# Attention and MLP on one core: a new written-out order of all work, and dummy matmuls of 256 columns

## The chip, the cores and the metric

The kernel runs on one core of a Trainium2 chip. The metric is the device time of one execution in microseconds (us). The core has five engines with instruction streams of their own: TensorE (PE in the profile, with its weight loads shown apart as PEld), VectorE (DVE), ScalarE (ACT), GpSimd (POOL) and SyncE (SP), which here only issues transfers. Transfers run on 16 DMA engines that all issuing engines share.

## The reference

```python
def phi(x):                          # sketch features, r = 8, so 64 of them
    a = einsum('rd,bhsd->bhsr', S1, x)
    b = einsum('rd,bhsd->bhsr', S2, x)
    return einsum('bhsi,bhsj->bhsij', a, b).reshape(*x.shape[:-1], r * r)

q_p, k_p = phi(q), phi(k)            # q, k, v: 4 batches, 4 heads, 1088 positions, 32 wide
kv  = einsum('bhsf,bhsd->bhfd', k_p, v)
z   = sum(k_p, axis=2)
num = einsum('bhsf,bhfd->bhsd', q_p, kv)
den = einsum('bhsf,bhf->bhs', q_p, z)[..., None] + 1e-06
x   = (num / den) as 4352 tokens x 128
h   = x @ w_in                       # 128 -> 2048
g   = maximum(h, 0) + alpha * minimum(h, 0)
out = g @ w_out                      # 2048 -> 128
```

Inputs and output are float32.

## The kernel before, in words

The kernel is one straight line of some 750 named steps (`Op`), each with an engine, and all of them stand in one string, `ORDER` (lines 23 to 67). A word such as `r0.4:a:2` says: step r0.4, on ScalarE (a; p is PE, d VectorE, g GpSimd, s SyncE), with buffer slot 2. A number behind the letter p (`rowsT:p4:6`) makes PE run so many dummy matmuls ahead of the step (`dummy`, line 293; called at line 781): 128 columns of ones, into a PSUM bank that nobody reads. `warm` (line 289) is 13 such matmuls of 256 columns at the very start. `arrange` (line 95) walks through ORDER; each engine takes its steps in that order, so ORDER decides what waits behind what. Each engine waits for the data and for the buffers that a step needs: PSUM has eight banks, "rh" (the activated hidden values) eight slots, "oT" (results on their way out) six.

The steps, by the names that follow:

- Loads: `ld_...` on SP, the four slices of w_in on GpSimd, and the small S1, S2, alpha on ScalarE. q and k come a batch at a time (544 KB), v in four parts per batch (`ld_v1`, `ld_v1_1` and so on), w_out in four slices. `winT0` to `winT3` (line 395) are transposing transfers of w_in inside the core.
- Weights: rowsT, Wk, Wf, S2m, S2q, Ssd prepare the sketch matrices; `w_a`, `w_b`, `w_hi`, `w_lo` scale and split w_out; `Wmm0` to `Wmm3` (line 404) multiply them with winT into W. The MLP is computed as relu(x w_in) times w_out (1 - alpha), plus x W.
- Keys of batch b: `k1T0` transposes, `k1f0` (line 491) makes features, `k1fT0` transposes back, `k1p0` and `k1p1` (helper at line 195) form the 64 products, `zs10` (line 517), `z11`, `zS1`, `C1` sum them up, `kv10` (line 530; batch 0: kv00 to kv04, line 546) multiplies them with v, `kvc1`, `fin1` (line 423) and `kvR1` lay the result out.
- Queries: batch 0 is split. Its first 512 columns take a short way of their own (`qaT`, `qaf` line 643, `qas`, `den` and `num` line 653, `dT`, `rc`, `rr`, `xA`). The rest, and batches 1 to 3, go through `qbT`/`q1T0`, `qbf`/`q1f` (line 448), `..fT`, `..t`, `..rc`, `..b`, `..p0`, `..p1`, `..PT0`, `..PT1`, `qbn`/`q1n` (line 607) and `..x0`, `..x1`, which write x.
- MLP: eleven groups of tokens (0, 1, 8, 9 and 10 have 256, the others 512). `h2.5` (line 702) is the matmul of group 2 with w_in slice 5, `r2.5` (ScalarE line 708 or VectorE line 710) evicts it with a relu, `o2.5` (line 723) multiplies with w_out, `W2` closes the sum (`D0` to `D2` do the x W part of groups 0 to 2 apart), `oT2` transposes the result, `st2` stores it (line 746: four transfers; line 753: eight). Group 10 is stored by `st10.0` on SP and `st10.1` on ScalarE (line 759).

A 256-token hidden step shares one eviction between two slices (r0.4 is for h0.4 and h0.5). Each PE matmul is two instructions, a weight load and a matmul; a matmul with float32 operands is passed through twice, so four. `qbn` for example has 128 instructions, `kv10` 144, a step h or o two.

## Time and profile before

| | us |
|---|---|
| runs of the kernel | 111.35, 111.72, 114.65 (median 111.72) |
| the profiled execution, time of its own | 112.21 |
| its span (first to last instruction) | 110.2 |
| PE busy in the span | 96.7 |
| VectorE, ScalarE, GpSimd busy | 80.5, 70.2, 46.7 |
| DMA: read and written in HBM | 8.80 MB, 2.23 MB |

The span is 2.0 us shorter than the execution, which has a start and an end around it. All engines overlap, so the busy times do not add up. Most loads fall in the first 36 us; the page's slices show the DMA engines full there, and nearly idle from 40 to 60 us. PE has 1401 weight loads (PEld) and 1401 matmuls. Start times below are counted from the span's start; a matmul's duration in the trace includes its way through the array, so that the spacing of starts is the price of one in a row.

### The profile page before, as it was taken

What the parts mean: (1) busy time and instruction counts of PE and PEld (TensorE: products, weight loads), DVE (VectorE), ACT (ScalarE), POOL (GpSimd) and SP (SyncE); (2) the same over time, 40 slices, a digit from 0 to 9 for tenths busy, and PEclk for the clock granted to TensorE, in tenths of its full rate; (3) what the DMA queues carried; (4) which work ended last, traced back from release to release, by engine and by line L of the source; (5) the groups of instructions that cost most, each with busy time, mean ns of one, the idle gap of its engine ahead of it and who ended that gap; (6) DMA issues with size and microseconds to landing.
All of it is one profiled execution on the core that took longest, in us unless ns stands there. A gap on an engine that the chain in (4) does not pass through costs nothing.

```text
span 110.2 us, 3417 instructions
## 1 busy us (share of the span) xinstructions
PE 96.7 (88%) x1401; PEld 56.5 (51%) x1401; DVE 80.5 (73%) x135; ACT 70.2 (64%) x150; POOL 46.7 (42%) x51
## 2 busy tenths in 40 slices
PE   7999999999169699999999999999999999999100
PEld 5638744687144346465444443446544466889100
DVE  4997979999349896997999978999946363857100
ACT  3304357989619779679679667395929979766000
POOL 7499009897205999370077039469300000000000
PEclk9999999999999999999999999999999999999955
DMA  3999999999999900000000500500112640551220
GB/s 68 300 258 270 238 295 312 239 143 295 239 180 312 77 6 0 6 0 0 6 0 0 95 0 6 95 1 6 24 30 38 120 81 3 98 102 32 44 43 23
DMA packets 26231, 11.25 MB, mean 102 GB/s; under 512 B 19928, under 2 KB 25064, under 8 KB 26216
## 3 DMA queue, kind: packets, MB, share of 16 engines
q1 hardware_dynamic: 25396, 10.43, 45.1%
q0 software_dynamic: 576, 0.52, 3.1%
q8 instruction: 11, 0.18, 0.7%
q10 hardware_dynamic: 244, 0.08, 0.3%
q14 instruction: 4, 0.03, 0.2%
HBM read 8.80 MB, written 2.23 MB: 100 GB/s over the span
## 4 chain that ended last, share of the span: by engine, by line
PE 71%; SPq 7%; issue 6%; DVE 5%; DMA 4%; ACT 1%; ACTq 0%; DVEq 0%
PE ps L723 23%; PE ps L702 23%; PE ps L607 5%; SPq L746 3%; PE ps L530 3%; SPq L753 3%; DMA k<-in_k_dram 3%; PE ps L448 2%; PE ps L491 2%; PE ps L546 2%; PE ps L517 2%; PE ps L643 2%; PE ps L404 2%; DMA out_dram<-oT__92 1%; PE ps L295 1%
## 5 line engine op out<-in xcount | busy, mean ns | idle before, releaser
L702 PE MATMUL ps<-x,w_in_bf 128*128 128x512 bf16 (+1 forms) x176 | 42.7, 331 | 0.5 <-DVE x L667 0.5
L702 PEld LDWEIGHTS <-w_in_bf 128*128 128x128 bf16 x176 | 16.9, 98 | 13.1 <-issue 1.1
L723 PEld LDWEIGHTS <-w_a_bf 128*128 128x128 bf16 x160 | 15.2, 98 | 15.6 <-issue 5.2
L195 POOL TENSOR_TENSOR P__71<-Fk__69 128x512 f32<-128x512 f32 (+3 forms) x7 | 12.1, 1747 | 5.4 <-DVE Fk__69 L496 5.4
L708 ACT ACTIVATE rh__84<-ps 128x512 bf16<-128x512 f32 x14 | 8.4, 597 | 3.8 <-PE ps L702 3.3
L723 PE MATMUL ps<-rh__85,w_a_bf 128*128 128x512 bf16 (+1 forms) x22 | 7.0, 331 | 3.2 <-issue 3.2
L708 ACT ACTIVATE rh__87<-ps 128x512 bf16<-128x512 f32 x13 | 7.9, 610 | 2.9 <-PE ps L702 2.0
L708 ACT ACTIVATE rh__83<-ps 128x512 bf16<-128x512 f32 x14 | 8.5, 605 | 1.6 <-PE ps L702 1.6
L708 ACT ACTIVATE rh__85<-ps 128x512 bf16<-128x512 f32 x14 | 8.4, 603 | 1.5 <-PE ps L723 1.2
L708 ACT ACTIVATE rh__86<-ps 128x512 bf16<-128x512 f32 x12 | 7.2, 600 | 1.9 <-PE ps L723 1.1
L723 PE MATMUL ps<-rh__83,w_a_bf 128*128 128x512 bf16 (+1 forms) x24 | 7.4, 335 | 0.0
L723 PE MATMUL ps<-rh__82,w_a_bf 128*128 128x512 bf16 (+1 forms) x21 | 7.3, 349 | 0.0
L708 ACT ACTIVATE rh__88<-ps 128x512 bf16<-128x512 f32 x10 | 6.1, 608 | 1.6 <-PE ps L702 1.2
L723 PE MATMUL ps<-rh__86,w_a_bf 128*128 128x512 bf16 (+1 forms) x21 | 7.0, 350 | 0.0
L708 ACT ACTIVATE rh__89<-ps 128x512 bf16<-128x512 f32 x11 | 6.7, 606 | 0.1
L708 ACT ACTIVATE rh__82<-ps 128x512 bf16<-128x512 f32 x11 | 6.7, 606 | 0.1
L195 POOL TENSOR_TENSOR P__71<-F__68 128x1152 f32<-128x1152 f32 x2 | 4.3, 2172 | 5.6 <-DVE F__68 L195 5.6
L195 POOL TENSOR_TENSOR w_hl<-w_b_f,w_hl 128x512 bf16<-128x512 f32 x4 | 5.8, 1473 | 1.8 <-ACT Wf L188 1.8
L727 DVE STREAM_TRANSPOSE oT__90<-ps 128x256 f32<-128x256 f32 (+1 forms) x4 | 2.3, 584 | 5.8 <-PE ps L723 5.8
L723 PE MATMUL ps<-rh__84,w_a_bf 128*128 128x256 bf16 (+1 forms) x20 | 6.2, 327 | 0.0
L607 PE MATMUL ps<-Q__74,kvR 32*32 32x288 f32 (+1 forms) x256 | 6.1, 385 | 0.0
L195 POOL TENSOR_TENSOR P__72<-F__67 128x640 f32<-128x640 f32 (+1 forms) x3 | 5.9, 1982 | 0.2
(176 smaller groups left out, 202.9 us busy)
## 6 DMA issues: line engine op xcount, KB each, us to landing
v<-in_v_dram SPq DMA_DIRECT2D x12, 144.0 KB, 6.8
k<-in_k_dram SPq DMA_DIRECT2D x3, 544.0 KB, 6.2
q<-in_q_dram SPq DMA_DIRECT2D x3, 544.0 KB
w_out_f<-in_moe_w_out_dram SPq DMA_DIRECT2D x4, 256.0 KB, 9.0
w_in_bf<-in_moe_w_in_dram POOLq DMA_DIRECT2D x4, 128.0 KB, 7.1
out_dram<-oT__90 SPq DMA_DIRECT2D x8, 64.0 KB, 1.9
v<-in_v_dram SPq DMA_DIRECT2D x4, 112.0 KB, 7.6
out_dram<-oT__93 SPq DMA_DIRECT2D x5, 64.0 KB, 1.9
```

The source lines that it names most:

```text
L195: (nc.vector if e == "dve" else nc.gpsimd).tensor_tensor(out=dst, in0=a, in1=b, op=what)
L404: nc.tensor.matmul(ps(bw)[:, :2 * DM], winT[:, c], w_hl[:, c].rearrange("p y m -> p (y m)"), start=c == 0, stop=c == NC - 1)
L448: nc.tensor.matmul(ps(bf)[32 * g:32 * g + 32, h, :n], Wf[32 * h:32 * h + 32, b], src[1]()[32 * h:32 * h + 32, g * n:(g + 1) * n], start=Tr ...
L491: nc.tensor.matmul(ps(bf)[32 * g:32 * g + 32, u, :n], Wk[K].rearrange("p x f -> p (x f)"), src[1]()[K, g * n:g * n + n], start=True, stop= ...
L530: nc.tensor.matmul(ps(bk)[32 * h:32 * h + 32, :R], v_sb[b][:, h, j], bview(sb(P), [[1, R]], (4 * j + h) * R), start=j == 0, stop=j == JG - ...
L607: nc.tensor.matmul(ps(bn)[32 * h:32 * h + 32, g, :n], kvR[b][32 * g:32 * g + 32, y, 32 * h:32 * h + 32], bview(sb(Q)[32 * g:32 * g + 32], ...
L702: nc.tensor.matmul(ps(b)[:, n * y:n * y + n], w_in_bf[:, c], x(), start=True, stop=True)
L708: nc.scalar.activation(sb(br), ps(b), ACTF.Relu)
L723: nc.tensor.matmul(ps(bo)[:, :n], w, y(), start=c == 0, stop=c == (NC - 1 if later else NC))
L727: o = op({"dve": V(n) + 40}, lambda e: nc.vector.transpose(sb(boT).rearrange("p j f -> p (j f)")[:, :n], ps(bo)[:, :n]), [last], [bo, boT] ...
L746: nc.sync.dma_start(bass.AP(tensor=out.tensor, offset=(b * S + lo // 32) * DM + 32 * i, ap=[[NJ * DM, 32], [DM, n // 32], [1, 32]]), t[32 ...
L753: nc.sync.dma_start(bass.AP(tensor=out.tensor, offset=(32 + y) * DM + 32 * i, ap=[[NJ * DM, 32], [S * DM, B], [1, 32]]), bview(t[32 * i:32 ...
```

## The change: ORDER is replaced, and dummies go in pairs

No step is added or removed apart from dummies, and no tile, shape or dependency is changed. The order in which the steps stand, the engine of 78 of them and the buffer slots are new. The dummy matmuls asked for fall from 16 to 9, and two of 128 columns are now one of 256:

```diff
     def dummy(n=1):
-        for _ in range(n):
-            nc.tensor.matmul(PS[:, 7, :128], ones(128), ones(128), start=True, stop=True, skip_group_check=True)
+        for i in range(0, n, 2):
+            m = 128 * min(2, n - i)
+            nc.tensor.matmul(PS[:, 7, :m], ones(128), ones(m), start=True, stop=True, skip_group_check=True)
```

Whole lines of the old and the new ORDER, from the parts that the prediction speaks of:

```diff
-ld_v0_3:s E8:d ld_alpha:a rowsT:p4:6 ld_qa1:s S2m:p:5 k0T0:d:0 Wk:a ld_qb:s ld_k1:s k0T1:d k0f0:p:0 gate:g ld_w_in0:g Wf:d M4:d qaT0:d ld_w_in1:g
-k0f1:p ld_w_out1:s S2q:d Ssd:d ld_w_in2:g ld_w_out0:s k0fT0:d:0 qaf0:p6:2 ld_w_in3:g k0fT1:d ld_w_out2:s zs00:p:6 k0p0:d:0 zs01:p ld_v1_2:s z10:a:0
-k0p1:d qas0:a zS0:p6 ld_v1:s kv00:p:1 k0p2:g zA:d:0 ld_w_out3:s qaT1:d zfin:p:0 C0:a kv01:p ld_q1:s zc:d:0 qaf1:p:2 qbT:d k0p3:g den0:p:6 ld_v1_1:s
+ld_v0_2:s k0T0:d:0 ld_v0_3:s rowsT:p4:6 ld_qa1:s Wk:d Wf:a gate:g k0T1:d I4:g k0f0:p4:0 ld_qb:s Ssd:d ld_w_in0:g ld_k1:s selP:d k0f1:p qaT0:d
+ld_w_in1:g ld_w_out1:s ld_w_in2:g qaf0:p:2 ld_v1_3:s k0fT0:d:0 ld_w_in3:g k0fT1:d ld_w_out0:s k0p0:d:0 ld_v1_2:s S2m:p1:6 qas0:a zs00:p:1 ld_q1:s
+k0p1:d zs01:p kv00:p:0 ld_v1_1:s k0p2:g zA:d:0 S2q:d kv01:p qaT1:d ld_v1:s zfin:p:6 qbT:d qaf1:p:2 k0p3:g zc:d:0 kv02:p ld_w_out2:s qas1:a k1T0:d:0
...
-zS1:p o0.10:p o0.11:p o1.5:p r1.14:a:6 C1:d o1.6:p o1.7:p k2T0:d:1 q1f:p:0 w_a3:a qbp1:g kv10:p:6 q1fT:d:1 r1.12:a:3 winT1:s o1.8:p o0.12:p o1.9:p
-kvc1:a:0 o1.10:p qbPT1:d o1.11:p w_hi1:a o0.13:p q1t:g:0 o1.12:p o1.13:p o1.14:p ld_v2_3:s o1.15:p w_b0:a fin1:p oT1:d:0 qbn:p:0 ld_q2:s q1rc:d:0
+ld_k3:s h1.0:p:4 r0.14:a:4 ld_q2:s qbrc:d:0 zs10:p:3 h1.1:p r0.12:a:5 o0.0:p:7 o0.1:p r0.6:d:6 ld_v2_2:s o0.2:p o0.3:p z11:a:0 h1.2:p:6 r1.0:a:7
+h1.3:p o0.4:p o0.5:p qbb:d r0.10:a:0 o0.6:p q1T0:d:0 o0.7:p qbp1:g:1 zS1:p h1.4:p:5 kv10:p:4 C1:a w_b2:a w_a2:g qbPT1:d:0 q1f:p:0 r1.2:a:1 kvc1:d:0
+qbp0:g w_hi2:a h1.5:p q1fT:d:1 fin1:p r1.4:a:3 h1.6:p:6 h1.7:p o0.8:p o0.9:p kvR1:a h1.8:p:5 r1.6:a:6 h1.9:p h1.10:p:4 qbPT0:d h1.11:p q1t:g:0
+h1.12:p:3 r1.8:a:2 h1.13:p winT1:s h1.14:p:2 h1.15:p o1.0:p:6 o0.10:p w_a3:g o1.1:p o0.11:p q1rc:d:0 o1.2:p o1.3:p r1.10:a:7 o1.4:p o1.5:p o1.6:p
+ld_v3_3:s r1.14:a:0 k2T0:d:0 w_b0:g o0.12:p o1.7:p r1.12:a:1 o0.13:p o1.8:p o1.9:p o1.10:p w_b3:a o0.14:p o0.15:p o1.11:p o1.12:p q1b:d o1.13:p
+qbn:p:0 oT0:d:0 q1p0:g:0 w_hi0:a k2f0:p:4 qbx0:d qbx1:a winT2:s h2.0:p:3 k2fT0:d:0 h2.1:p:2 q1p1:g h2.2:p:1 r2.0:a:1 h2.3:p:0 r2.2:d:2 h2.4:p:5
```

SP's transfers, old and new order, with the parts of v left under one name where they stand together: before k0, qa0, v0, qa1, qb, k1, w_out1, w_out0, w_out2, v1_2, v1, w_out3, q1, v1_1, v1_3, k2, v2_2, winT0, v2, v3_2, k3, winT1, v2_3, q2, winT2, v3, v3_3, q3, v2_1, winT3, v3_1, then the stores st3, st4, st1, st5, st2, st0, st6 to st10.0; after k0, qa0, v0, qa1, qb, k1, w_out1, v1_3, w_out0, v1_2, q1, v1_1, v1, w_out2, w_out3, k2, winT0, k3, q2, v2_2, winT1, v3_3, winT2, winT3, v3, v3_2, q3, v2_1, v2, v2_3, st2, st3, v3_1, st4, st5, st0, st1, st6 to st10.0.

Steps that change their engine, in the parts spoken of: Wk, C0, kvc1, qbb, k2p1, w_hi1, w_lo1 and w_hi3 go to VectorE, Wf, r0.0 and C1 to ScalarE, k2p0 and I4 to GpSimd.

## The prediction

> **What bounds the kernel now.** I read the page first, then a table of the span in stages, then TensorE's waits, then its instructions around each wait, then the DMA queues, and last SyncE's stores. In the rows of the stage table the columns after the stretch and its length are busy time (and instructions) of PE, PEld, DVE, ACT, POOL, then granted clock, DMA share and GB/s.

> ```profile
> PE 96.7 (88%) x1401; PEld 56.5 (51%) x1401; DVE 80.5 (73%) x135; ACT 70.2 (64%) x150; POOL 46.7 (42%) x51
> ...
> 16.43:28.07 11.64, 11.39 (x255) 7.78 (x255) 10.98 (x18) 10.47 (x28) 10.10 (x9) 1.00 1.22 248
> 28.07:31.23 3.16, 0.00 (x1) 0.00 (x0) 0.34 (x1) 1.25 (x5) 0.49 (x1) 1.00 1.00 249
> 31.23:38.25 7.02, 6.04 (x129) 3.17 (x128) 6.27 (x11) 4.96 (x10) 4.06 (x2) 1.00 1.16 184
> 38.25:102.40 64.15, 64.15 (x799) 35.72 (x798) 49.84 (x68) 47.56 (x95) 23.45 (x16) 1.00 0.19 32
> 102.40:110.20 7.80, 0.00 (x0) 0.00 (x0) 0.29 (x1) 0.27 (x1) 0.00 (x0) 0.66 0.18 37
> ```

> TensorE has no idle time from 38.25 to 102.40, and 0.25 us of it in the 11.64 us before 28.07. What is left is one hole of 3.16 us, one of 0.98 us (7.02 less 6.04), the start, and 7.8 us of stores behind the last matmul. PE ends when its work plus its holes are done. Both holes are put down to "issue", that is to nothing that another engine did:

> ```profile
> PE ps L723 <- issue: 3.2, 1, 3.2
> PE ps L517 <- issue: 1.0, 1, 1.0
> ...
> 23.91 0.27 PE L723 MATMUL ps<-rh__88,w_a_bf 128*128 128x256 bf16 x1
> 31.23 0.27 PE L723 MATMUL ps<-rh__85,w_a_bf 128*128 128x256 bf16 x1 [3.16 <-issue]
> 38.25 0.26 PE L517 MATMUL ps<-Fk__69 128*32 128x16 f32 x8 [0.98 <-issue]
> ...
> q8 instruction: 11, 0.18, 0.7%
> ```

> When is a block asked for? If it is when PE enters the block before, then 692 (o0.8, the row at 23.91) to 31.23 is 7.3 us and 31.23 to 38.25 is 7.0 us. The DMA view counts PE's packets of that time in the stretches 19.2 to 19.3, 27.9 to 28.0 and 35.4 to 35.5:

> ```profile
> q8 instruction: 1, 0.02, 88.8%
> ...
> q8 instruction: 1, 0.02, 115.4%
> ...
> q8 instruction: 1, 0.02, 81.7%
> ```

> So a packet shows 4.0 and 4.2 us after the crossing, and PE goes on 3.3 and 2.85 us after that. All this lies in the time in which the DMA engines are full (share 1.00 to 1.22).

> **Prices.**

> ```profile
> 15.46 0.71 PE L565 MATMUL ps<-kv0W,I 64*128 64x128 f32 x4
> 16.43 0.38 PE L702 MATMUL ps<-x,w_in_bf 128*128 128x256 bf16 x2 [0.27 <-DVE x L667]
> 17.31 0.57 PE L448 MATMUL ps<-qTb,Wf 32*32 32x160 f32 x32
> 19.02 1.25 PE L702 MATMUL ps<-x,w_in_bf 128*128 128x256 bf16 x10
> 21.39 0.50 PE L517 MATMUL ps<-Fk__69 128*32 128x16 f32 x36
> 25.27 0.77 PE L448 MATMUL ps<-T__64,Wf 32*32 32x288 f32 x32
> 25.97 1.23 PE L530 MATMUL ps<-P__71,v 128*32 128x64 f32 x72
> 31.86 1.27 PE L607 MATMUL ps<-Q__74,kvR 32*32 32x160 f32 x64
> 33.06 0.72 PE L491 MATMUL ps<-T__65,Wk 64*32 64x288 f32 x16
> 33.83 0.38 PE L702 MATMUL ps<-x,w_in_bf 128*128 128x512 bf16 x1
> 34.16 1.89 PE L702 MATMUL ps<-x,w_in_bf 128*128 128x512 bf16 x8
> ```

> From start to start: a 256-column matmul 0.109, a 512-column one 0.215; qbf 0.5, q1f 0.7, k2f0 0.65, zs 0.45, kv 1.16 (144 instructions), qbn 1.2 (128 instructions). The short ones are what empties a block fast: kv10 alone is over half a block in 1.16 us.

> **The change, part by part.**

> *Where the blocks end.* Counting the new ORDER the same way gives 2780 instructions (5 dummy matmuls for 16). I keep the bounds at the same numbers. Bound 436 is then at the start of qbf, 692 a quarter into kv10, 948 in the first tenth of qbn, 1204 near the end of zs20. PE's own work between them:
> 436 to 692: qbf 0.5, num1 0.57 (as den and num in before), 27 matmuls of 256 columns 2.94, zs10 0.45, zS1 0.2, 34/144 of kv10 0.27: 4.9.
> 692 to 948: rest of kv10 0.89, q1f 0.7, fin1 0.2, 33 of 256 columns 3.6, a tenth of qbn 0.1: 5.5.
> 948 to 1204: rest of qbn 1.1, k2f0 0.65, 27 of 512 columns 5.8, 54/72 of zs20 0.34: 7.9.
> Before, the second of these took 4.16 us (23.91 to 28.07), the third 6.04. So q1f and kv10 no longer share a block with little else.

> *The start.* In the chain of waits PE runs on from 5.25 to 13.9, and two groups of six dummies lie in it:

> ```profile
> 5.25 1.22 PE ps L491 x16
> 6.47 0.75 PE ps L295 x6
> ...
> 9.04 0.62 PE ps L295 x6
> ...
> 13.90 0.22 ACT kv0W L557
> ...
> 4.38 0.77 PE L356 MATMUL ps<-rows,selP 16*128 16x128 f32 x2
> 7.15 1.24 PE L643 MATMUL ps<-qTa,Ssd 32*128 32x256 f32 x8
> 11.28 0.71 PE L643 MATMUL ps<-qTa,Ssd 32*128 32x256 f32 x8
> L295 PE MATMUL ps<-const-bfloat16-1.0 x5: 218/281/314, 9.1 to 9.4; 128*128 128x128 bf16 x5
> ```

> Gone are 1.37 us, less 0.1 for the one dummy left there; S2m comes into this stretch (at most 0.5 of its 0.77, the rest overlaps); zS0 goes between num0 and fin0 (0.15). That alone is -0.6. Against it: qaf0 takes 1.17 us at 7.15 and 0.65 at 11.28, and the dummies' records shorten to 218 ns at 9.4, though the granted clock reads 1.00 throughout. So PE came to full speed at 9.4, 4.1 us after its last gap, at 5.25. The dummies that are gone covered the wait of qaf0 for VectorE (qaT0 now stands behind Ssd and selP); I estimate the new gap to end at 6.5, and full speed then at 10.6. Each us at the low speed loses 1 - 0.65/1.17 = 0.44, so 1.25 us cost 0.55. Sum -0.1; bounds -0.6 (no later speed) and +0.8 (3.2 us later). h0.0, at 16.43 before, comes at 16.3; h0.0, h0.1 and den1 stand ahead of qbf as before (17.31 less 16.43), so bound 436 is crossed at 17.2.

> *The blocks.* The block for 692 was asked for at 15.9 before (fourth matmul of fin0), its packet shows at 19.2, 3.3 later, and nothing waited for it. With 3.3 to go on after the packet it needs 6.6; bounds 6.2 (3.3 + 2.85) and 7.5 (4.2 + 3.3). Crossing 692: 17.2 + 6.6 = 23.8. PE's work alone would bring it there at 22.1, but kv10 also waits for k1's products on GpSimd and for evictions, so the wait seen will be about 1. The next block was seen twice, 7.3 and 7.0; I take 7.0: crossing 948 at 30.8, where before had 31.23: **-0.4**. The least would be 23.8 + 5.5 = 29.3. The block for 1204 comes at 37.8, PE needs it at 30.8 + 7.9 = 38.7: no hole, **-1.0**. Cover 0.9; without it the hole is back.

> *Work left after 948.* Before, o0.14, o0.15, o1.13 (3 x 0.109), fin1 (0.2) and a tenth of qbn were still to come there; now they are done: **-0.65**. Everything else behind 948 is the same work.

> *Loads, engines, queues.* The same transfers are issued on the same queues, SP's with k3, q2 ahead of most of v2 and v3; k2, w_out and v1 stay early, and v2 is needed by kv20, some 8 us behind bound 1204, where the DMA share is 0.19. v3_1 goes behind st2 and st3 on SP, with st2 waiting for GpSimd's oA2; only kv30, over 15 us later, needs it. Evictions on VectorE are 37 before and after; w_hi1, w_lo1, w_hi3 and k2p1 go to it, k2p0 leaves it. DVE is at 49.84 of 64.15 us behind 38.25. PE now runs some 2 us ahead there, with less cover: **+0.2** for new waits, bounds 0 and 1.

> *The stores.* W6 comes 2 us earlier, W7 0.3 later, W8 and W9 as before, counted from PE's end. SyncE is busy without a break from st7 on and sets the last store:

> ```profile
> 93.32 1.94 SPq L746 DMA_DIRECT2D out_dram<-oT__90  x4
> 95.37 2.36 SPq L746 DMA_DIRECT2D out_dram<-oT__91  x4
> 97.84 4.46 SPq L753 DMA_DIRECT2D out_dram<-oT__92  x8
> 102.40 3.58 SPq L746 DMA_DIRECT2D out_dram<-oT__90  x4
> ```

> st7, st8, st9 follow one another as before, so the 7.8 us stay: 0.

> Sum: -0.4 - 1.0 - 0.65 + 0.2 = -1.85. The profiled execution took 112.21 us (span 110.2 and 2.0 around it), so 110.4; against the median of the three runs, 111.72, it is **109.9 us**.

> **Rivals.** About 2% is what a measurement of this kernel can tell from no change: 109.5 and 114.0.
> 1. *The blocks come sooner* (bytes in flight differ, no hole left): 17.2 + 4.9 + 5.5, plus 0.25 of small waits as in 16.43 to 28.07, puts 948 at 27.9; -3.3 - 1.65 + 0.2 = -4.8, 107.0. Half of it gives 108.4. For it: the first two packets show after 3.3, not 4. Against: the DMA share is 1.0 and more there. Chance 0.30 for 109.4 and less by this.
> 2. *SyncE's last group shortens.* st9's four stores took 3.58, st6's 1.94; if the 1.64 goes, 108.2. No rule for it in the trace. 0.12.
> 3. *The holes are not blocks*, and move along unchanged: -0.1 + 0.2, about 111.8. [...] 0.08.
> 4. *Slower: full speed comes late.* Fewer dummies leave PE gaps from 6 to 16 us, and if none of that runs at full speed, the 6.8 us of work between 9.4 and 16.4 take 1.17/0.65 as long: +5.4, h0.0 at 21.2, bound 948 at 35.7 (22.1 + 6.6 + 7.0): +4.5 - 1.65 + 0.2, 114.8. It decides from h0.0 at 20.5. Against it: behind the one gap PE has work in a row. [...] 0.14 with other waits of that size.

> Forecast 0.36. Faster by over 2%: 1 and 2, 0.42. Slower: 0.14. Within: 0.44. The range goes from rival 1 nearly whole, 107.1, to the sum with its upper bounds: h0.0 at 17.2, 948 at 18.1 + 7.5 + 7.3 = 32.9, new waits 1: +1.7 - 1.65 + 1.0 = +1.1, 112.8.

> **What would show it.** Holes put down to "issue" in kv10 (under 1.5 us) and in qbn (1 to 1.6), none in zs20; PE's records at full length until about 10.6; h0.0 at 16.3, h2.0 near 32.6 (30.8 + 1.1 + 0.65; 33.83 before); 7.8 us behind PE's end. A hole elsewhere by "issue" breaks the count; waits on DVE or ACT behind 38 us break the 0.2; h0.0 behind 18 breaks the start.

## The result, and the profile after

The changed kernel took 107.73 us at the median of four executions (106.83 to 111.37) against 112.03 for the kernel before on the same chip: ratio 0.961, 95% interval 0.951 to 0.971. In a second set of runs it was 109.13 against 112.28, 0.972 (0.956 to 0.988). It is faster in both, though only the first interval lies wholly beyond 2%; the prediction had 109.9 with a range from 107.1 to 112.8. Executions of one program differ here in how long TensorE stays at low speed at the start: in the execution of 111.37 us, which was the one profiled, its records keep about double length until 23.5 us, so below the profile of the second set is read (an execution of 107.37 us, the fastest of that set, span 105.6).

The table of the span in stages, of the changed kernel, cut at PE's holes and waits; columns as before (busy time of PE, PEld, DVE, ACT, POOL, then granted clock, DMA share, GB/s):

```profile
15.06:19.90 4.84, 2.89 (x57) 1.18 (x56) 4.44 (x7) 2.54 (x7) 3.39 (x2) 1.00 1.10 274
19.90:23.99 4.09, 3.78 (x83) 2.78 (x82) 3.81 (x8) 3.62 (x10) 3.71 (x4) 1.00 1.46 259
23.99:31.50 7.51, 6.97 (x185) 5.07 (x185) 6.11 (x9) 6.44 (x16) 5.70 (x7) 1.00 1.07 235
31.50:40.00 8.50, 8.46 (x159) 3.93 (x143) 7.58 (x9) 6.83 (x15) 8.50 (x6) 1.00 0.75 155
40.00:97.00 57.00, 57.00 (x703) 30.73 (x673) 46.06 (x67) 40.24 (x79) 18.59 (x12) 1.00 0.21 37
```

The 3.16 and 0.98 us without any PE work are gone. From 31.5 on PE has 0.04 us of idle time; before, it had none from 38.25 on. The largest hole is new and lies in the first row, where PE worked 2.89 of 4.84 us. TensorE's waits name it, and its instructions place it:

```profile
PE ps L703 <- DVE F__67 L452: 1.9, 1, 1.9
PE ps L724 <- POOL w_a_bf L195: 0.4, 1, 0.4
PE ps L531 <- issue: 0.3, 1, 0.3
```

```profile
6.38 0.71 PE L644 MATMUL ps<-qTa,Ssd 32*128 32x256 f32 x8 [0.22 <-DVE qTa L635]
15.06 0.38 PE L703 MATMUL ps<-x,w_in_bf 128*128 128x256 bf16 x2 [0.23 <-DVE x L668]
15.94 0.57 PE L449 MATMUL ps<-qTb,Wf 32*32 32x160 f32 x32
19.90 1.14 PE L703 MATMUL ps<-x,w_in_bf 128*128 128x256 bf16 x9 [1.95 <-DVE F__67 L452]
23.16 0.52 PE L531 MATMUL ps<-P__71,v 128*32 128x64 f32 x18
23.99 0.98 PE L531 MATMUL ps<-P__71,v 128*32 128x64 f32 x54 [0.31 <-issue]
30.61 0.41 PE L608 MATMUL ps<-Q__74,kvR 32*32 32x160 f32 x14
32.37 1.89 PE L703 MATMUL ps<-x,w_in_bf 128*128 128x512 bf16 x7
99.82 0.28 PE L721 MATMUL ps<-W_bf,x 128*128 128x128 bf16 x2
```

qaf0 is already at full length at 6.38 (0.71 us; before, 1.24 at 7.15). The block bound at 692 shows: kv10 stops after 18 of its 72 matmuls (a quarter, instruction 694) and is continued after 0.31 us by "issue". qbn, with bound 948 in its first tenth, starts at 30.61 without a hole. PE's last matmul ends at 100.10, 2.3 us sooner than before (102.40).

The other part of the gain is behind PE. SyncE's stores at the end, changed kernel:

```profile
92.96 1.96 SPq L747 DMA_DIRECT2D out_dram<-oT__91  x4
95.02 4.76 SPq L754 DMA_DIRECT2D out_dram<-oT__90  x8
99.88 1.85 SPq L747 DMA_DIRECT2D out_dram<-oT__91  x4
101.83 0.71 SPq L760 DMA_DIRECT2D out_dram<-oT__93  x1
```

st9 (99.88) takes 1.85 us instead of 3.58, so the span ends 5.5 us behind PE instead of 7.8. Together 4.6 us of span: 2.3 in PE, 2.3 behind it.

That split is one pair of executions. The part behind PE is steady: 7.5 to 7.9 us in four profiles with the old order, 5.5 to 6.0 in six with the new one, as long as the stores are left as they are. PE's part is not: with full speed by 10.2 us and kept from there, PE ended at 102.40, 102.29 and 100.82 under the old order with its loads (the last is the run with a store's slot moved, below), and between 99.05 and 101.22 in five profiles of the new one. How much of the gain at the median is PE's stays open.

### The profile page after: what moved, and what is told of

Read it like the earlier page. It is cut to its first block, busy times and chain, and to the rows that moved or that the text cites. A ratio compares the mean times of both kernels' runs of the same rounds, so it can differ in the third digit from the quotient of the medians.

```text
span 109.5 us, 3387 instructions
## 1 busy us (share of the span) xinstructions
PE 101.1 (92%) x1380; PEld 58.3 (53%) x1390; DVE 79.3 (72%) x137; ACT 66.1 (60%) x137; POOL 49.0 (45%) x55
## 4 chain that ended last, share of the span: by engine, by line
PE 84%; DMA 3%; issue 3%; DVE 2%; POOL 2%; ACT 1%; ACTq 1%; DVEq 0%; POOLq 0%
PE ps L703 26%; PE ps L724 25%; PE ps L608 5%; PE ps L547 4%; PE ps L492 4%; PE ps L654 4%; PE ps L531 3%; DMA rows<-in_S_dram 3%; PE ps L449 3%; PE ps L644 2%; PE ps L518 2%; PE ps L405 2%; DVE F__68 L452 1%; PE ps L566 1%; POOL w_a_bf L195 1%
## 5 line engine op out<-in xcount | busy, mean ns | idle before, releaser
L703 PE MATMUL ps<-x,w_in_bf 128*128 128x512 bf16 (+1 forms) x174 | 43.8, 333 | 0.4
L709 ACT ACTIVATE rh__82<-ps 128x512 bf16<-128x512 f32 x14 | 8.5, 605 | 4.4 <-PE ps L703 3.7
L709 ACT ACTIVATE rh__85<-ps 128x512 bf16<-128x512 f32 x14 | 8.4, 603 | 4.3 <-PE ps L703 3.6
L709 ACT ACTIVATE rh__87<-ps 128x512 bf16<-128x512 f32 x15 | 8.9, 597 | 0.7 <-PE ps L703 0.6
L709 ACT ACTIVATE rh__86<-ps 128x512 bf16<-128x512 f32 x11 | 6.6, 604 | 3.3 <-PE ps L703 1.9
L709 ACT ACTIVATE rh__84<-ps 128x512 bf16<-128x512 f32 x14 | 8.4, 602 | 0.3 <-PE ps L724 0.3
L709 ACT ACTIVATE rh__88<-ps 128x512 bf16<-128x512 f32 x13 | 7.8, 603 | 0.4 <-PE ps L724 0.3
L711 DVE TENSOR_SCALAR rh__83<-ps 128x512 bf16<-128x512 f32 x8 | 5.5, 690 | 3.2 <-PE ps L703 1.8
L709 ACT ACTIVATE rh__83<-ps 128x512 bf16<-128x512 f32 x10 | 6.1, 608 | 2.4 <-PE ps L703 2.2
L724 PE MATMUL ps<-rh__85,w_a_bf 128*128 128x512 bf16 (+1 forms) x20 | 6.6, 348 | 0.3 <-issue 0.3
L724 PE MATMUL ps<-rh__83,w_a_bf 128*128 128x512 bf16 (+1 forms) x22 | 6.6, 331 | 0.2 <-issue 0.2
L724 PE MATMUL ps<-rh__84,w_a_bf 128*128 128x512 bf16 (+1 forms) x21 | 6.6, 338 | 0.0
L724 PE MATMUL ps<-rh__87,w_a_bf 128*128 128x512 bf16 (+1 forms) x18 | 6.0, 344 | 0.4 <-POOL w_a_bf L195 0.4
L195 POOL TENSOR_TENSOR w_a_bf<-w_out_f,omaT 128x512 bf16<-128x512 f32 x3 | 3.1, 1041 | 7.0 <-DVE omaT L366 7.0
L724 PE MATMUL ps<-rh__89,w_a_bf 128*128 128x256 bf16 (+1 forms) x19 | 5.7, 323 | 0.0
L195 POOL TENSOR_TENSOR F__67<-F__67,rd__78 128x288 f32<-128x288 f32 x2 | 1.4, 682 | 9.5 <-DVE rd__78 L594 9.5
L724 PE MATMUL ps<-rh__82,w_a_bf 128*128 128x256 bf16 (+1 forms) x18 | 5.5, 320 | 0.0
```

Of the source, the lines that this page charges most:

```text
L195: (nc.vector if e == "dve" else nc.gpsimd).tensor_tensor(out=dst, in0=a, in1=b, op=what)
L703: nc.tensor.matmul(ps(b)[:, n * y:n * y + n], w_in_bf[:, c], x(), start=True, stop=True)
L709: nc.scalar.activation(sb(br), ps(b), ACTF.Relu)
L711: nc.vector.tensor_scalar_max(sb(br), ps(b), 0.0)
L724: nc.tensor.matmul(ps(bo)[:, :n], w, y(), start=c == 0, stop=c == (NC - 1 if later else NC))
```

## The experiments

### The change as it stands, once more

No edit.

> The changed kernel as it is, to have its trace with PE at full speed early. Block theory: no wait put down to issue above 0.5 us in kv10, qbn or zs20, PE's end some 4 us before 102.4 and the same 7.8 us behind it, so a span near 105 to 106. Rival (the holes are tied to the moment at which the loads run, 28 to 31 us in, not to the instruction count): a hole of 2 to 3 us near 28 to 31 us, wherever PE stands then, and the gain comes from the start and the stores.

This is the run read above.

### Single dummies

```diff
-        for i in range(0, n, 2):
-            m = 128 * min(2, n - i)
-            nc.tensor.matmul(PS[:, 7, :m], ones(128), ones(m), start=True, stop=True, skip_group_check=True)
+        for _ in range(n):
+            nc.tensor.matmul(PS[:, 7, :128], ones(128), ones(128), start=True, stop=True, skip_group_check=True)
```

> The changed kernel with its nine dummies as nine matmuls of 128 columns again: the same columns, 4 matmuls (8 instructions) more, so the block bounds come 8 instructions earlier. If only the order matters: within 0.3 us of the changed kernel. If the pairs are what matters (for the speed of PE or for the bounds): 1 us or more apart.

107.49 us, ratio 0.964 (0.952 to 0.977), beside 0.972 (0.956 to 0.988) for the pairs on the same chip. The median is 1.6 us lower, but the intervals overlap: no difference that can be measured. The gain doesn't hang on the pairs; it belongs to the order.

### The same order, 82 instructions later

```diff
     def warm(e):
-        for _ in range(WARM):
-            nc.tensor.matmul(PS[:, 7, :256], ones(128), ones(256), start=True, stop=True, skip_group_check=True)
+        for _ in range(54):
+            nc.tensor.matmul(PS[:, 7, :62], ones(128), ones(62), start=True, stop=True, skip_group_check=True)
```

54 short matmuls for 13 long ones, 82 instructions more and nearly the same columns, 3348 for 3328. Everything behind them is the changed kernel; only the block bounds fall elsewhere.

> The changed kernel with the 13 warming matmuls of 256 columns cut into 54 of 62: nearly the same columns (3348 for 3328), but 82 instructions more ahead of all work, the order of the work untouched. Block theory: the bounds move 82 instructions earlier in the work, to 354, 610, 866, 1122; kv10 and q1f then lie in one block (610 to 866), whose work is 4.2 us; a hole put down to issue of 1.5 to 3 us at or next to h1.5, and a time 1 to 2.5 us above the changed kernel. Rival (moment of the loads): no hole, within 0.4 us of it.

111.76 us, ratio 1.000 (0.992 to 1.009): the whole gain is gone. PE's instructions at its holes:

```profile
15.03 0.69 PE L492 MATMUL ps<-T__64,Wk 64*32 64x288 f32 x8 [1.91 <-issue]
29.39 0.27 PE L703 MATMUL ps<-x,w_in_bf 128*128 128x256 bf16 x1 [1.68 <-issue]
```

The first stands after half of k1f0, instruction 360 of the changed count (436 less 82 is 354), the second ahead of h1.5, instruction 866, which is 948 less 82. TensorE's records also went back to double length behind the first hole, with a granted clock of 0.50 from 15.8 to 22.7 us. Where h1.5 was ready to start, at 27.7, PE was 2.1 us behind the changed kernel (25.61); the second hole added 1.7. So the loss is in part lost speed. Behind PE the stores' part stayed (6.0 us); PE's end, 103.73, was later than in the kernel before. That the holes stand at the bounds is shown; that the whole loss is theirs is not.

### The kernel before with paired dummies

The change of `dummy` alone, in the kernel before: 16 instructions fewer ahead of the holes.

> The kernel before with its 16 dummies in pairs: 8 matmuls for 16, so 16 instructions fewer ahead of the work. Block theory: both holes stay near 3.2 and 1.0 us but move 16 instructions later in the work: the first from ahead of o1.13 to qbn's second matmul call (instruction 964 of the old count), the second from zs20 to h2.11; time within 0.5 us of before. Rival (moment of the loads): the first hole stays ahead of o1.13 or o1.14. If the pairs alone make the gain: 2 us or more faster.

113.76 us (112.12 to 114.86), where the kernel before had 112.28 (110.40 to 115.67) on the same chip: no gain, and not the "within 0.5 us" of the expectation. The holes:

```profile
30.78 1.14 PE L608 MATMUL ps<-Q__74,kvR 32*32 32x160 f32 x61 [1.58 <-issue]
38.34 0.59 PE L703 MATMUL ps<-x,w_in_bf 128*128 128x512 bf16 x2 [2.21 <-issue]
```

Both moved by 16 instructions: the first from ahead of o1.13 to three matmuls into qbn, the second from zs20 to h2.11. The holes hang on a count, not on a step. Their sizes did not stay: 1.58 and 2.21 us for 3.16 and 0.98.

### The wait at the start: where the addition's operand lies

The new 1.95 us ahead of h0.8 go back to one VectorE instruction, rc1's addition of 1e-6, which took 2.32 us (0.18 in rc0) and ended with a product on GpSimd that had begun just before it:

```profile
13.51 0.18 DVE L663 TENSOR_SCALAR dt<-dt 128x8 f32<-128x8 f32 x1
16.56 2.32 DVE L663 TENSOR_SCALAR dt<-dt 128x8 f32<-128x8 f32 x1
16.46 2.39 POOL L195 TENSOR_TENSOR P__71<-Fk__69 128x1280 f32<-128x1280 f32 x1
```

```diff
-nc.vector.tensor_scalar_add(dt[:, :, 2], dt[:, :, 0], EPS)
+nc.vector.tensor_tensor(out=dt[:, :, 2], in0=dt[:, :, 0], in1=epsT, op=ALU.add)
```

(epsT is a constant tile of 128 x 8.)

> The changed kernel with the addition of 1e-6 in rc0 and rc1 written as tensor plus a constant tile in place of tensor plus a number. In a1_changed this addition took 2.32 us in rc1 (0.18 in rc0) and ended with GpSimd's k1p0, and PE stood still for 1.95 us ahead of h0.8. Theory (the form of the instruction makes it wait for GpSimd's running one): rc1's addition takes 0.2 to 0.3 us, the PE wait ahead of h0.8 goes. What is late next by the block theory: the block for instruction 692 in kv10, which came at 23.99; so a hole put down to issue of 1.5 to 2.3 us in kv10, and a time only 0 to 0.5 us under the changed kernel. Rival (the addition waits for GpSimd in either form): no change in the trace there.

```profile
15.13 0.17 DVE L665 TENSOR_TENSOR dt<-dt,epsT 128x8 f32<-128x8 f32 x1
18.18 1.70 DVE L665 TENSOR_TENSOR dt<-dt,epsT 128x8 f32<-128x8 f32 x1
20.90 1.14 PE L705 MATMUL ps<-x,w_in_bf 128*128 128x256 bf16 x9 [1.33 <-DVE F__67 L454]
```

The theory fell: the addition is held in either form, 1.70 us of it here. 108.17 us, 0.976 (0.956 to 0.996). In three traces the addition of a number ended 0.03 us behind the GpSimd product that had begun before it: the 2.32 us above at 18.88 (the product at 18.85), 0.42 us in the execution of 111.37 us at 22.79 (22.76), and 0.42 us in the run with the dummies back, below, at 17.33 (17.30). Why it waits for the product is not shown.

### The dummies back ahead of qaf0 and zs00

```diff
-qaf0:p:2 ... zs00:p:1
+qaf0:p6:2 ... zs00:p6:1
```

> The changed kernel with six dummies ahead of qaf0 and six ahead of zs00 again, in pairs: 11 x 0.107 us more PE work in the start and 10 instructions more ahead of bound 180. If the dropped dummies are part of the gain: 0.7 to 1.2 us slower than the changed kernel, h0.0 near 16. If the start is covered by what waits behind it (rc1, which ends with GpSimd's product, and the block in kv10): within 0.4 us. If the dummies bring PE to full speed sooner and more surely: full speed by 6.5, and the runs lie closer together than the changed kernel's 106.8 to 111.4.

108.23 us, 0.976 (0.964 to 0.988), four executions within 0.95 us of each other. The 1.95 us ahead of h0.8 did not arise, and yet PE ended at 100.44:

```profile
22.80 0.42 PE L531 MATMUL ps<-P__71,v 128*32 128x64 f32 x12 [0.61 <-DMA v<-in_v_dram]
24.22 1.09 PE L531 MATMUL ps<-P__71,v 128*32 128x64 f32 x60 [1.01 <-issue]
```

kv10 took over: it waited for v, then 1.01 us for its block. So in this execution PE follows the block of bound 692 up to 24 us, and what is saved ahead of it comes back as a longer hole. The hole stands after 12 of kv10's matmuls where the changed kernel had it after 18: six dummy matmuls more, twelve instructions, so the count holds here too.

### A store's slot in the kernel before

In the kernel before, st9 stands 1.9 us among its four stores, and SyncE's waits put that down to a transfer of another queue: that of the tile oT__91, which ScalarE's st10.1 stores (issued at 103.10):

```profile
SPq L746 <- DMA out_dram<-oT__91: 1.9, 1, 1.9
```

In the execution of 111.37 us of the changed kernel st9 has no such wait (1.86 us for its four stores), and st10.1 stores oT__92 there. That the tile's slot decides which store waits was the author's estimate. The edit, in the kernel before:

```diff
-oT10.1:a:1
+oT10.1:a:4
```

> The kernel before with one number changed: oT10.1 in slot 4 in place of slot 1. [...] Theory: SyncE's hole of 1.9 us between st9's third and fourth store goes, PE's end stays at 102.4, the rest behind it falls from 7.8 to 5.5 to 6.1 us, 1.7 to 2.3 us faster than before. Rival (the hole is the DMA engines being busy): it stays, within 0.4 us.

113.05 us, 1.021 (1.005 to 1.037): no gain. SyncE's stores, then the wait in st8, PE's two holes and its last matmul:

```profile
96.19 8.17 SPq L753 DMA_DIRECT2D out_dram<-oT__92  x8
104.46 1.86 SPq L746 DMA_DIRECT2D out_dram<-oT__90  x4
```

```profile
SPq L753 <- DMA out_dram<-oT__94: 3.6, 1, 3.6
29.93 0.27 PE L723 MATMUL ps<-rh__85,w_a_bf 128*128 128x256 bf16 x1 [1.52 <-issue]
36.68 0.26 PE L517 MATMUL ps<-Fk__69 128*32 128x16 f32 x8 [0.80 <-issue]
100.54 0.28 PE L720 MATMUL ps<-W_bf,x 128*128 128x128 bf16 x2
```

st9's hole is gone (1.86), and st8, which took 4.46, takes 8.17: it now waits 3.6 us for the transfer of st10.1 (now of tile oT__94). The wait moved from st9 to st8 with the slot, and is put down to the same transfer of ScalarE's queue in both; full DMA engines are not its cause (share 0.27 in the kernel before from 102.40 to 106.08). Why a store waits there for another queue's transfer is not shown; that the edit would gain was wrong. What the steady 2 us behind PE are worth alone in the kernel before was not measured.

The two rows of PE's holes matter for what follows. Up to its last store this is the order of the kernel before, with all its loads, and yet the hole ahead of o1.13 is 1.52 us for 3.16: from the crossing of 692 (24.24) the block took 5.7 us, not 7.3, and PE ended 1.6 us sooner. One execution against another is worth that much.

### st9 on GpSimd, and two sums

```diff
-st9:s
+st9:g
```

> The changed kernel with st9's four stores issued by GpSimd, which has nothing else to do then, in place of SyncE. In a1_changed SyncE is busy without a break from st7 on and issues st10.0 at 101.83, 1.4 us after its data. Theory (SyncE's queue sets the end): st10.0 0.3 to 0.4 us behind PE's end, 1 to 1.5 us off the span behind PE's end (5.5 to some 4.2). Rival: GpSimd's own stores land last, no gain.

106.83 us, 0.962 (0.949 to 0.976). In the profiled execution PE ends at 101.60 and the span at 106.7, 5.1 us behind it where the changed kernel had 5.5; the gain is smaller than the expected 1 us and more. SyncE's last store, and the end of the chain of waits, which says what is late next:

```profile
101.95 0.71 SPq L760 DMA_DIRECT2D out_dram<-oT__93  x1
```

```profile
100.47 1.83 POOL out_dram L747 x3
102.30 0.57 POOLq L808
```

SyncE is out of the way (its st10.0 comes 0.35 us behind PE's end, at 101.95, where it came 1.7 behind before the edit), and now GpSimd's own four issues, 2.4 us of them from 100.47 on, are the last thing in the chain.

Two sums of the parts followed: this with the dummies back, and this with single dummies.

> The changed kernel with both: the six dummies back ahead of qaf0 and of zs00, and st9 issued by GpSimd. If the two parts add up: PE ends near 100.2, the span ends 5.1 us behind it, 107 to 107.5 us at the median with a spread under 1.5. Rival: the dummies move the end of the block that kv10 crosses (a hole near 1 us, as when they were put back alone) and nothing is left of the cover: 108.2 as then.

> The changed kernel with single dummies of 128 columns (as before) and st9 issued by GpSimd. Theory (neither the pairs nor the wait at the start set PE's end, the order does; the store's queue gives some tenths): 106.5 to 107.2 at the median. Rival: no sum, 107.5.

107.73 us, 0.964 (0.956 to 0.971), and 107.48, 0.955 (0.944 to 0.966). The intervals of all these overlap with the changed kernel's 0.951 to 0.971. None is shown to beat it. Nor do the dummies make full speed early: the first of the two sums, which has them, took 113.02 us in the execution that was profiled, with double-length records until about 27 us.

### Fewer loads in the way

In the prediction the delivery of a block was a number, 7 us, put beside full DMA engines without a test. The kernel before again, with ten loads later (k3, q2, q3, three parts of v2, all of v3), first issued by GpSimd between its products:

```diff
-... winT0:s ... ld_v2:s ... ld_v3_2:s ... ld_k3:s ... ld_v2_3:s ... ld_q2:s ...
+... q1p0:g:0 ld_v2:g ld_q2:g ... q1p1:g ld_v2_3:g ld_v2_1:g ld_k3:g ... k2p1:g:1 ld_v3:g ld_v3_3:g ld_q3:g ld_v3_2:g ld_v3_1:g ...
```

> The kernel before, with ten loads (k3, q2, q3, three parts of v2, the four of v3; some 2.6 MB) taken from SyncE's early queue and issued by GpSimd behind q1p0, q1p1 and k2p1 (from about 36 us on). PE's order is that of before, so the blocks end at the same instructions (o1.13, zs20). Theory (a block is asked for when PE enters the one before, and is 7 us on its way because the DMA engines are full): with less queued, the packet of the block for 948 shows under 3.5 us after 692 and the hole ahead of o1.13 shrinks from 3.16 to under 1.5 us; the hole in zs20 is under 0.3; PE reaches h2.0 2 to 4 us sooner. Rival A (delivery takes about 7 us whatever the load): both holes stay at 3.2 and 1.0 within 0.5. Rival B (the loads are needed earlier than they now come): new waits on DMA ahead of kv20, q2T0 or k3T0 give the gain back, and the time is no better than before though the holes are smaller.

112.44 us, 1.010 (1.006 to 1.014). The profiled execution took 116.06, with double-length records until 23.9, so only what lies behind is read. For that early part its row, in the columns of the stage table, is:

```profile
6.85:23.92 17.07, 17.07 (x231) 9.76 (x231) 10.88 (x25) 5.76 (x17) 7.33 (x7) 0.50 0.99 253
```

The granted clock was 0.50 there, with PE busy all the time. Stage table from the crossing of 692 on, and PE's waits:

```profile
28.58:32.58 4.00, 4.00 (x131) 2.87 (x129) 3.67 (x5) 3.86 (x11) 2.32 (x3) 1.00 0.51 41
```

```profile
PE ps L404 <- POOL w_hl L195: 1.9, 3, 1.3
...
PE ps L434 <- DVE z__98 L190: 0.7, 1, 0.7
PE ps L530 <- DMA v<-in_v_dram: 0.5, 1, 0.5
```

The whole block of 256 ran through without idle time and into the next, where the kernel before stood 3.16 us. The packet showed 0.4 to 0.5 us behind the crossing (29.0 to 29.1), before 4.0. Both holes are gone. PE also came to this crossing 4.7 us later than before, for want of speed, so the loads had more time to end; the edit alone was not seen at full speed. Of their 4.1 us, 3.1 came back as the three waits above, mostly for w_hl products that stand behind 5.7 us of DMA issues on GpSimd (5.2 in the expectation). So theory and rival B both held, one for the holes, the other for the time.

The execution of the changed kernel that took 111.37 us shows the same without any edit to the loads. It crossed bound 436 at 21.75, when the early loads were ending: the next packet showed at 22.12, 0.4 us later, where the execution read above, which crossed at 15.94 with the loads going on, had it at 21.50. kv10 had no hole by "issue" there.

To spare GpSimd, the last run kept the loads on SyncE and held them with a one-element copy:

```diff
+    loads["v2"][0].deps.append(op({"pool": 120}, lambda e: nc.gpsimd.tensor_copy(v_sb[2][:1, 0, 0, :1], ident[:1, :1]), lat=LG, name="gate2"))
```

> The kernel before with the same ten loads late, but still on SyncE: a one-element copy on GpSimd behind q1p0 (0.1 us; the load of v2 overwrites that element) holds SyncE back until then, so that GpSimd's products aren't delayed. PE's order is that of before. Theory (with the loads out of the way the blocks come in time, 0.4 us behind the crossing as in the run with the loads on GpSimd; what ate the gain there were GpSimd's issues, 5.2 us of them, ahead of the w_hl products): no hole by issue in o1.13 and zs20, 4.1 us less; new waits on v2 or on winT3 under 1 us; 107.8 to 109.3 us at the median, ratio 0.965 to 0.98. Rival (the loads themselves come too late, or contend with what runs from 36 to 46 us): holes gone, but waits on DMA ahead of kv20, q2T0, k3T0 or Wmm of 3 us and more, 111 to 112.

In the profiled execution (109.82 us, span 107.9), from the crossing of 692 on, the stage table and PE's instructions:

```profile
23.87:28.03 4.16, 4.16 (x130) 2.86 (x128) 3.83 (x5) 4.02 (x12) 3.27 (x3) 1.00 0.58 72
...
28.72:34.23 5.51, 5.46 (x99) 2.75 (x99) 4.83 (x10) 4.20 (x10) 2.61 (x3) 1.00 0.02 4
```

```profile
28.72 0.27 PE L724 MATMUL ps<-rh__85,w_a_bf 128*128 128x256 bf16 x1 [0.69 <-issue]
34.23 0.50 PE L517 MATMUL ps<-Fk__69 128*32 128x16 f32 x36
40.69 1.21 PE L530 MATMUL ps<-P__72,v 128*32 128x64 f32 x72 [1.11 <-DMA k<-in_k_dram]
99.72 0.28 PE L721 MATMUL ps<-W_bf,x 128*128 128x128 bf16 x2
```

The same row of the kernel before, for the load in that block:

```profile
23.91:28.07 4.16, 4.16 (x130) 2.86 (x128) 3.83 (x5) 4.02 (x12) 3.27 (x3) 1.00 1.20 246
```

The same work of 4.16 us, with a DMA share of 0.58 for 1.20: the hole ahead of o1.13 shrinks to 0.69 from 3.16 (from 1.52 in the run with a store's slot moved), and zs20 runs through. The packet was counted at 25.4, 1.5 us behind the crossing, and PE went on 3.3 behind that, as in the kernel before (3.3), though hardly a load was moving by then (17 GB/s and less from 25.5 on). So the loads in the queue made the packet late (4.0 us behind the crossing before, 1.5 here); the time from there to PE's going on was 3.3 us with loads and nearly without (2.5 in the changed kernel, from 21.50 to 23.99). A new wait of 1.11 us for k stands ahead of kv20. PE ended at 100.00, about as in the changed kernel, with the old order. The time at the median did not follow: 112.14 us over twelve executions (109.82 to 117.39), 1.006 (0.995 to 1.018), against the 107.8 to 109.3 expected. The execution with the rows is the fastest of the twelve, and the kernel before had executions down to 108.85 on that chip, so a gain in time is not shown. Of the longer ones there are no rows: why the smaller holes didn't show in the time stays open.

## Why the prediction was right, and where it was not

**The blocks.** Holes by a count of 256: right (moved by 16 with 16 instructions, by 82 with 82). The forecast's bounds 436, 692, 948 and 1204 were where the new order had them; holes in kv10 (0.31; under 1.5 expected) and none in zs20 as said.

**The crossings.** Two steps were off and cancelled, which is luck. Bound 436 was crossed at 15.94, not 17.2. Its successor was then on its way 8.05 us, to 23.99, where the prediction took 6.6 with an upper bound of 7.5: a crossing that comes sooner meets the same queue of loads (DMA share 1.12 until the packet showed, at 21.50). The step that failed is the delivery as a fixed time from the crossing on: where PE waited under full loads it was 7.3 and 7.0 us in the kernel before, 5.7 with a store's slot moved and 8.05 here, with the loads gated 4.9, and at a crossing at which the loads were ending the packet came 0.4 us behind it. So 692 came at 23.99 for 23.8, 948 at 30.7 or so for 30.8. But the hole of 1 to 1.6 us in qbn did not come: PE's own way from 692 to 948 took 6.6 us, not the 5.5 of the sum (0.36 of it a wait for w_a, and eight of the hidden steps 0.15 us apart instead of 0.109), and the block was there by then.

**The start.** Forecast -0.1, h0.0 at 16.3: measured 15.06, -1.4, beyond the bound of -0.6. The gap ahead of qaf0 came where it was put (to 6.38, for 6.5); the step that failed is full speed 4.1 us behind it, at 10.6: the row at 6.38 has full length already. The prediction's remark that the granted clock reads 1.00 throughout, low speed or not, was a misreading: the trace's list of granted clocks begins only at 9.38 in the kernel before, where the prediction puts full speed, at 5.57 in this execution and at 23.66 in that of 111.37 us, and what lies ahead of its first entry reads 1.00 in the rows. The earlier start gave nothing in the end: h0.8 waited 1.95 us for the slowed addition, and with that wait gone kv10 waited for its block instead. Rival 4, full speed late, is what the execution of 111.37 us showed. Three of its instructions of PE:

```profile
14.17 1.08 PE L654 MATMUL ps<-aq,zc 128*32 128x256 f32 x8
20.20 0.61 PE L703 MATMUL ps<-x,w_in_bf 128*128 128x256 bf16 x2
23.91 0.83 PE L703 MATMUL ps<-x,w_in_bf 128*128 128x256 bf16 x6
```

h0.0 came at 20.20, just short of the 20.5 from which that rival decides, and only from 23.91 on are six matmuls of 256 columns 0.11 apart. The reason that it gave, gaps, is not the one: PE has no idle time there from 4.74 on. Work without a break did not bring full speed by itself: here it came only after 18.92 us of it (4.74 to 23.66), and in the run with late loads PE was busy through 17.07 us at a granted clock of 0.50. What decides it in an execution stays open.

**From 948 to PE's end.** -1.0 (no hole at 1204), -0.65 (work moved ahead) and +0.2 make -1.45; from 30.65 to 100.10 it took 69.45, before from 31.23 to 102.40 71.17: -1.7. No new wait behind 31.5, so the +0.2 was 0. PE in all: -2.3 for -1.85, against one execution of the kernel before; against the one that ended at 100.82 it would be -0.7. The sum for PE is borne out in kind, not to a tenth.

**The stores.** This is the term that failed: 0, with 7.8 us behind PE's end, measured 5.5. Rival 2 (0.12) was the true one, on top of the forecast instead of in its place: 1.7 of the 2.3 us are st9's hole, and what the prediction missed in the trace is st9's wait of 1.9 us for the transfer of ScalarE's last store. "SyncE is busy without a break from st7 on" was a misreading: 1.9 us of st9's 3.58 are a wait, and "no rule for it in the trace" overlooked the line of SyncE's waits that names it. Of the rest, 0.2 is that st9 starts 0.2 us ahead of PE's end and no longer with it, and 0.35 that less follows the last issue. With it, the forecast's 109.9 would have read 108.2; the measured medians are 107.73 and 109.13. So a good part of the gain came by a way that the sum had at nothing.

**Rivals 1 and 3.** The blocks came no sooner (8.05 and 6.7 us at most for 7), but rival 1's reason, that the bytes in flight decide, is borne out: with fewer loads in the way the packet came in 0.4 to 1.5 us. Rival 3 falls: the holes moved with the count, by 16 and by 82 instructions. A crossing left no hole where the 256 instructions lasted longer than the delivery, which under full loads took 5.7 to 8.05 us in the profiles named above.

## What to carry to other kernels

Count the instructions of the engine that bounds a kernel. Here the idle time by "issue" that moved with the count (by 16 and by 82 instructions) was a block on its way; longer instructions in the block closed one hole (0.98 us in zs20), and fewer loads in the way of the next shrank the other (3.16 us to 0.69). Closing the hole is not yet a gain: two runs here closed or shrank both and were no faster at the median. Six dummy matmuls moved such a hole by twelve instructions, and 82 instructions more took the whole gain away (1.000 for 0.972), so that a gain that seems to be a better order may be 80 instructions' worth of luck. One profile against one profile is not enough for a split of the gain: the same order of TensorE's work differed by 1.6 us in its end. Where an issuing queue stands in the middle of a row of stores, look for the transfer that it waits for, on the other queues too: here it stood 1.9 us for one of ScalarE's.

## What was not expected of the hardware

- A store on SyncE stood 1.9 us for the transfer of ScalarE's last store, and when that store's slot was changed, another stood 3.6 us for it (st8 took 8.17 for 4.46).
- A VectorE addition of 128 x 8 took 2.32 us beside a GpSimd product of 2.39, in the other form 1.70, alone 0.18.
- The start of full TensorE speed differs between executions of one program: by 6.4 us in one, about 23.5 in another. It was lost again in three runs: behind a hole of 1.91 us at 13.1 the granted clock was 0.50 from 15.8 to 22.7 (the run 82 instructions later), behind a wait of 1.93 us at 18.5 from 22.0 to 25.5 (st9 on GpSimd), and in the run with late loads from 6.9 to 23.9 while PE was busy.
- From an instruction packet's record to PE's going on, where it stood waiting, it was 3.3 and 2.8 us in the kernel before, 2.5 in the changed kernel and 3.3 with the loads gated, when hardly a load was moving. The packet's own delay went with the loads in the queue: 0.4 to 1.5 us behind the crossing where they were ending, over or gated (the execution of 111.37 us, the late loads, the gated loads), 4.0 and 4.2 us in the kernel before and 5.6 in the changed kernel, where they went on.
